# First batch by the casting software queue, four of its masks as copy and select, its last k scaled on POOL

## The chip, the cores and the metric

One core of a Trainium2 chip. The metric is device microseconds (us) of an execution. Before the change it was 208.72 us, the median of 3 runs (208.58 to 209.14). A ratio is the mean time of one kernel's fast runs over the mean time of the other's from the same rounds on the same chip, so it is not quite the ratio of the medians that are quoted beside it.

PE is the matrix engine, PEld its weight loads, DVE the vector engine, ACT the scalar engine, POOL the GpSimd engine and SP the engine that issues the hardware queue's transfers. L400 is line 400 of the kernel that the profile is of; the line numbers differ from kernel to kernel.

## The reference

```python
# q, k, v: (4, 8, 768, 64), float32
for t in range(S):                                   # retention, per batch and head
    state = gamma * state + outer(k[t], v[t])
    y[t] = scale * q[t] @ state
x = y.transpose(0, 2, 1, 3).reshape(B, S, H * D)     # (4, 768, 512)
h = np.maximum(x.transpose(0, 2, 1) @ w_tok1, 0.0) @ w_tok2
u = x + h.transpose(0, 2, 1)                         # token mixing
out = u + np.maximum(u @ w_ch1, 0.0) @ w_ch2         # channel MLP
```

## The kernel before

Each batch has four head pairs. The front of a pair loads k, q and v (384 KB of float32 each), scales k and casts q and v to float16, transposes k and q on PE, computes the attention of chunks of 128 in two halves, masks it, adds the state, and does the token mixing. The back of a batch is the channel MLP. The weights are cast on their way by the software queue (POOL): two for the token mixing, then the first channel weight in two pieces, c1a and c1b, then the second channel weight, c2.

```python
# loads: all by the hardware queue, and batch 1 waits for c1b
dma = nc.sync.dma_start(out=t, in_=rows.rearrange("h (c p) d -> p (h c) d", p=P))
if b == 1:
    tc.add_manual_dep(dma.ins, wops["c1", 1].ins.ins.name, ...,   # [cut]
                      reason="the weights come first")
# ... k scaled on DVE, q and v cast on POOL ...
nc.vector.tensor_scalar(k16[:, :, j, :], src, gk[:, h:h + 1], None, ALU.mult)
nc.gpsimd.tensor_copy(t.rearrange("p c h d -> p h c d"), src.tile...)   # [cut]
# ... attention of one half into two PSUM banks, then the mask ...
nc.vector.tensor_tensor(am, src[:, :HC], mask, ALU.mult)
```

The order of the work is not the order of this text. A list scheduler in the kernel (`arrange`) simulates all engines with assumed durations, and the instructions of each engine are emitted in the order that it finds. PE executes them in that order, whatever is ready.

PSUM has eight banks, five for `fa` tiles and three for `ba` tiles. A bank is free when its last reader has read it: for an attention half the reader is the mask on DVE.

Of the kernel before, what the change touches and what calls it, by code (L numbers as in the profile page):

```python
# [17 lines left out]
def kernel(  # L18
# [13 lines left out]
    P = 128  # L32
# [42 lines left out]
    make_identity(nc, ident16)  # L75

    gp = const_p.tile([P, NP], FP, name="gp")
    for p in range(NP):
# [4 lines left out]
    nc.gpsimd.affine_select(  # L83
        out=mask, in_=mask, compare_op=ALU.is_ge, fill=0.0,
        base=0, pattern=[[0, HC], [1, P]], channel_multiplier=-1,
    )
# [12 lines left out]
    BUFS = dict(kf=4, qf=4, vf=4, k16=3, q16=3, v16=4, kT=4, qT=4, U=3, am=8, x16=2, h1=4, u16=3, u16w=2,  # L99
# [3 lines left out]
    LONG, XK, XQ, XU, XBAR, RING = 2, 2, 2, 2, 1500, 3  # L103
# [18 lines left out]
    def arrange():  # L122


        way = {}
        for op in reversed(ops):
            if op.first is not None:
                way[op] = way.get(op, 0) + op.lat + SEM
                for d in op.deps:
                    way[d] = max(way.get(d, 0), way[op])  # L130
        for op in ops:
            if op.first is not None:
                op.prio = (op.prio[0], 0, EARLY * op.first - way[op], op.first)
        free = dict(PE=5000, ACT=5000, DVE=4600, POOL=4000, SP=1300, DMA=1300)
        taken = {t: [] for t in BUFS}
        todo, order, ring = list(ops), [], []
        while todo:
            best = []
            for op in todo:
                if any(d.end is None for d in op.deps):  # L140
                    continue
                start = free[op.eng]
                if op.dma and op.eng == "SP" and len(ring) >= RING:
                    start = max(start, ring[-RING])
                for d in op.deps:
                    if d.eng == op.eng and (d.dma or d.eng == "PE"):
                        continue
                    start = max(start, d.end + (30 if d.eng == op.eng else SEM) + op.guard)
                more = {}
                for s in op.takes:  # L150
                    q = taken[s.tag]
                    n = len(q) + more.get(s.tag, 0) - BUFS[s.tag]
                    more[s.tag] = more.get(s.tag, 0) + 1
                    if n >= 0:
                        old = q[n]
                        if any(u.end is None for u in old.users):
                            break
                        start = max([start] + [u.end + SEM for u in old.users])
                else:
                    best.append((start, op))  # L160
            t = min(b[0] for b in best)

            eng = min(best, key=lambda b: (b[0], b[1].prio))[1].eng
            start, op = min((b for b in best if b[1].eng == eng and b[0] <= t + 20),
                            key=lambda b: b[1].prio)
            free[op.eng] = start + op.occ
            op.start = start
            if op.dma:
                free["DMA"] = max(free["DMA"], start + 50) + op.dma
                op.end = free["DMA"] + 1600  # L170
                if op.eng == "SP":
                    ring.append(free["DMA"])
            else:
                op.end = start + op.lat
            for s in op.takes:
                taken[s.tag].append(s)
            todo.remove(op)
            order.append(op)
        return order
# [16 lines left out]
    def weight(key, ns, out, src, dep):  # L196
        def emit():
            return nc.gpsimd.dma_start(out=out, in_=src.rearrange("(i p) j -> p i j", p=P))
        wops[key] = Op("POOL", (0,) if key in ("t1", "t2", ("c1", 0)) else (1, 0, 99), 800, 800, emit, deps=[dep], dma=ns)


    load_done = [None]
# [4 lines left out]
    def front(b, p):  # L207
# [20 lines left out]
        sl, ld = {}, {}  # L228
        for nm, src in (("k", k), ("q", q), ("v", v)):
            sl[nm] = Slot(nm + "f")  # L230

            def emit(nm=nm, src=src):
                t = tile_of(sl[nm], sb, [P, 2 * NC, D], FP)
                rows = src[b, 2 * p:2 * p + 2]
                if nm == "q" and b < LONG:

                    dma = nc.sync.dma_start(  # L237
                        out=t.rearrange("p (h f i) d -> p h f (i d)", h=2, f=2),
                        in_=rows.rearrange("h (f p i) d -> p h f (i d)", f=2, p=P))
                else:  # L240
                    dma = nc.sync.dma_start(out=t, in_=rows.rearrange("h (c p) d -> p (h c) d", p=P))  # L241
                if b == 1:
                    tc.add_manual_dep(
                        dma.ins, wops["c1", 1].ins.ins.name,
                        mybir.DependencyInfo(mybir.DependencyClass.Sync, mybir.DependencyReason.DATA),
                        reason="the weights come first")
            ld[nm] = Op("SP", (0, b, p), 100, 100, emit,
                        deps=[load_done[-1]] + ([wops["c1", 1]] if b == 1 else []),
                        takes=[sl[nm]], dma=1200 if nm == "q" and b < LONG else 1750)
            load_done.append(ld[nm])  # L250

        K, Q, V = Slot("k16"), Slot("q16"), Slot("v16")

        def emit():
            k16 = tile_of(K, sb, [P, NC, 2, D], F16)
            for j in range(2):
                h = 2 * p + j
                src = sl["k"].tile[:, j * NC:(j + 1) * NC, :]
                if KENG == "ACT":
                    nc.scalar.mul(k16[:, :, j, :], src, gk[:, h:h + 1])  # L260
                else:
                    nc.vector.tensor_scalar(k16[:, :, j, :], src, gk[:, h:h + 1], None, ALU.mult)  # L262
        KENG = "DVE"
        kc = op(KENG, 900, 980, emit, [ld["k"]], [K], [sl["k"]])

        def cast(slot, src):
            def emit():
                t = tile_of(slot, sb, [P, NC, 2, D], F16)
                nc.gpsimd.tensor_copy(t.rearrange("p c h d -> p h c d"),  # L269
                                      src.tile.rearrange("p (h c) d -> p h c d", h=2))  # L270
            return emit
        qc = op("POOL", 770, 830, cast(Q, sl["q"]), [ld["q"]], [Q], [sl["q"]])
        vc = op("POOL", 770, 830, cast(V, sl["v"]), [ld["v"]], [V], [sl["v"]])
        KT, QT = Slot("kT"), Slot("qT")

        def turn(src, dst, dep, eng):
            T = Slot("fa")

            def emit():
                T.tile = tp = tile_of(T, ps, [P, 512], FP).bitcast(F16)  # L280
                for c in range(NC):
                    nc.tensor.transpose(tp[:, c * P:(c + 1) * P],  # L282
                                        src.tile[:, c].rearrange("p h d -> p (h d)"), ident16)
# [11 lines left out]
        def crossbar(src, dst, dep):  # L295
            def emit():
# [3 lines left out]
                    in_=src.tile.rearrange("p c h d -> p (c h d)"))  # L300
# [7 lines left out]
        def emit():  # L308
            st = tile_of(ST, ps, [P, 512], FP)
            for c in range(NC - 1):  # L310
                for j in range(2):
                    nc.tensor.matmul(st[j * D:(j + 1) * D, c * D:(c + 1) * D], K.tile[:, c, j],  # L312
                                     V.tile[:, c, j], start=True, stop=True)
# [20 lines left out]
        def emit():  # L334
            nc.vector.tensor_scalar(RS.tile[D:, :, D:], US.tile[D:], g128[2 * p + 1], None, ALU.mult)
        r1 = op("DVE", 400, 480, emit, [prev, r0], [], [US, RS])
# [4 lines left out]
        for hf in range(2):  # L341
# [12 lines left out]
            for j in range(2):  # L354
                def emit(hf=hf, j=j, A=A):
                    am = tile_of(AM[2 * hf + j], sb, [P, HC, P], F16)
                    src = A[j].tile.rearrange("p (i t) -> p i t", t=P)
                    nc.vector.tensor_tensor(am, src[:, :HC], mask, ALU.mult)  # L358
                am_ops.append(op("DVE", 470, 550, emit, [a], [AM[2 * hf + j]], [A[j]]))
        X16 = Slot("x16")  # L360
        x_ops, xf = [], []
        for hf in range(2):
            Y = Slot("fa")

            def emit(hf=hf, Y=Y):
                y = tile_of(Y, ps, [P, 512], FP)
                R = RS.tile
                for i in range(HC):
# [5 lines left out]
                    for j in range(2):  # L374
                        nc.tensor.matmul(o[:, j * D:(j + 1) * D], AM[2 * hf + j].tile[:, i],  # L375
                                         V.tile[:, c, j], start=(c == 0), stop=(c == 0 or j == 1))
# [51 lines left out]
        t1 = op("PE", 690, 860, emit, x_ops + [wops["t1"], None if first else t2_done.get(b * NP + p - 1)], [T1], [X16])  # L428
# [10 lines left out]
        for hf in range(2):  # L439
# [9 lines left out]
            t2 = op("PE", 350, 520, emit, [hr, wops["t2"]], [T2], [H1])  # L449
# [64 lines left out]
    def back(b):  # L514
# [6 lines left out]
        for sh in range(2):  # L521
# [26 lines left out]
            for i in range(HC):  # L548
# [3 lines left out]
                for part in range(parts):  # L552
# [25 lines left out]
                    op("SP", 100, 100, emit, [ad], [], [O]).dma = 800 // parts  # L578


    weight("t1", 2000, wt1, moe_w_tok1, None)
    weight("t2", 2000, wt2, moe_w_tok2, None)
    for i, (f0, f1) in enumerate(CUT1):
        weight(("c1", i), 650 * (f1 - f0), wc1[i], moe_w_ch1[:, f0 * P:f1 * P], None)
    weight(("c2", 0), 7800, wc2, moe_w_ch2, None)
    casts = [front(0, p) for p in range(NP)]
    after = {"t1": casts[2][2], ("c1", 0): casts[3][1]}
    last = None
    for key, o in wops.items():
        o.deps += [d for d in (after.get(key), last) if d is not None]  # L590
        last = o

    for b in range(1, B):
        for p in range(NP):
            front(b, p)
    for b in range(B):
# [40 lines left out]
```

## Time and profile before

| kernel before | |
|---|---|
| time, median | 208.72 us |
| profiled span | 206.8 us |
| first channel matmul (end of the head) | 38.08 us |
| PE busy from there to the last matmul | 164.83 of 165.22 us |
| padding matmuls, all in the head | 62 |

### The profile page before, as it was taken

To read this page: it belongs to the slowest core of one execution; us is meant where nothing else is said; L and a number is where in the kernel's file an instruction comes from. 1 tells how busy PE (TensorE), PEld (TensorE's weight loads), DVE (VectorE), ACT (ScalarE), POOL (GpSimd) and SP (SyncE) were. 2 spreads that over 40 slices of the span, in tenths; PEclk is the share of its full clock that TensorE was granted. 3 is DMA by queue.
4 is the path that set the end of the run, shared out by engine and by line. 5 is a ranking of instruction groups with operands and counts; after the bars stand their busy time and mean duration, and the time that the engine had idled before them with its cause. 6 is when DMAs were issued, how large, how long until landed. Compare 5 with 4: busy or idle time off the path is not lost.

```text
span 206.8 us, 4738 instructions
## 1 busy us (share of the span) xinstructions
PE 198.9 (96%) x1898; PEld 120.5 (58%) x1898; DVE 114.8 (56%) x291; ACT 96.2 (47%) x205; POOL 61.9 (30%) x107
## 2 busy tenths in 40 slices
PE   6899899999999999999999999999999999999993
PEld 2554487564667667576656574458556545545552
DVE  6377896114998878996794726686663021021021
ACT  7237458674497842455502670176215604604600
POOL 2338852113345635252533134115311000000000
PEclk9999999999999999999999999999999999999999
DMA  6999999999999999989995899996722012012012
GB/s 165 248 244 247 188 207 201 202 263 237 295 271 213 189 203 230 226 177 162 212 171 141 145 216 218 155 263 107 152 101 75 17 51 101 3 51 101 0 54 101
DMA packets 92790, 34.13 MB, mean 165 GB/s; under 512 B 81888, under 2 KB 89312, under 8 KB 92768
## 3 DMA queue, kind: packets, MB, share of 16 engines
q1 hardware_dynamic: 89104, 29.89, 72.6%
q0 software_dynamic: 3664, 3.93, 11.4%
q8 instruction: 15, 0.25, 0.5%
q14 instruction: 7, 0.06, 0.1%
HBM read 26.74 MB, written 6.29 MB: 160 GB/s over the span
## 4 chain that ended last, share of the span: by engine, by line
PE 83%; SPq 5%; DMA 4%; DVE 3%; ACT 2%; issue 1%; POOL 0%; DVEq 0%
PE ba L532 31%; PE ba L561 29%; PE fa L426 4%; DMA kf<-in_k_dram 4%; PE fa L447 4%; PE fa L351 3%; SPq L241 3%; PE fa L375 3%; SPq L237 2%; PE fa L372 2%; PE fa L282 2%; PE fa L312 2%; DVE k L262 1%; PE ba L426 1%; PE ba L189 1%
## 5 line engine op out<-in xcount | busy, mean ns | idle before, releaser
L532 PE MATMUL ba<-uT,wc 128*128 128x384 f16 x384 | 68.4, 326 | 0.0
L561 PE MATMUL ba<-wc,h 128*128 128x512 f16 (+1 forms) x300 | 67.7, 371 | 0.0
L545 ACT ACTIVATE h<-ba 128x384 f16<-128x384 f32 x96 | 46.7, 490 | 41.3 <-PE ba L532 40.4
L532 PEld LDWEIGHTS <-wc 128*128 128x128 f16 x384 | 35.5, 98 | 22.2
L570 DVE TENSOR_TENSOR o<-x,ba 128x512 f32<-128x512 f32 (+1 forms) x25 | 16.6, 663 | 50.1 <-PE ba L561 49.7
L561 PEld LDWEIGHTS <-h 128*128 128x128 f16 x300 | 27.6, 98 | 27.0
L358 DVE TENSOR_TENSOR am<-fa,mask 128x384 f16<-128x384 f32 x64 | 32.7, 550 | 5.3 <-PE fa L351 4.8
L403 POOL CAST x<-x 128x384 f16<-128x384 f32 x30 | 15.0, 512 | 37.6 <-issue 20.4
L269 POOL CAST q<-qf 128x768 f16<-128x768 f32 x16 | 13.7, 854 | 29.3 <-DMA qf<-in_q_dram 24.7
L386 ACT ACTIVATE x<-fa,gy 128x192 f32<-128x192 f32 (+1 forms) x42 | 15.1, 417 | 9.2 <-PE fa L375 8.7
L262 DVE TENSOR_SCALAR k<-kf,gk 128x384 f16<-128x384 f32 x32 | 14.5, 495 | 7.6 <-DMA kf<-in_k_dram 7.5
L189 PE MATMUL fa<-zero 128*128 128x512 f16 x54 | 15.9, 425 | 2.4 <-DVE zero L52 1.3
L331 ACT ACTIVATE r<-U 64x320 f16<-64x320 f32 x16 | 7.4, 465 | 23.2 <-DVE U L324 23.2
L324 DVE SCALAR_TENSOR_TENSOR U<-U,gp,fa 128x64 f32<-128x64 f32 x64 | 17.1, 275 | 1.0
L454 DVE TENSOR_TENSOR x<-x,fa 128x384 f32<-128x384 f32 x24 | 12.5, 549 | 6.3 <-POOL q L269 3.1
L291 ACT COPY qT<-fa 128x768 f16<-128x768 f16 x8 | 11.6, 1455 | 6.5 <-PE fa L282 6.5
L269 POOL CAST v<-vf 128x768 f16<-128x768 f32 x16 | 13.2, 827 | 4.6 <-DMA vf<-in_v_dram 3.7
L375 PE MATMUL fa<-v,am 128*128 128x64 f16 x192 | 13.9, 193 | 0.0
L375 PEld LDWEIGHTS <-am 128*128 128x128 f16 x192 | 12.1, 98 | 1.9
L426 PEld LDWEIGHTS <-wt 128*128 128x128 f16 x192 | 11.7, 98 | 2.6 <-issue 0.4
L447 PEld LDWEIGHTS <-wt 128*128 128x128 f16 x192 | 11.8, 98 | 2.0
L465 POOL CAST u16w<-x 128x384 f16<-128x384 f32 x16 | 7.9, 506 | 14.7 <-DVE x L454 14.6
(53 smaller groups left out, 164.3 us busy)
## 6 DMA issues: line engine op xcount, KB each, us to landing
kf<-in_k_dram SPq DMA_DIRECT2D x16, 384.0 KB, 6.5
qf<-in_q_dram SPq DMA_DIRECT2D x16, 384.0 KB, 6.1
vf<-in_v_dram SPq DMA_DIRECT2D x16, 384.0 KB, 5.8
out_dram<-o SPq DMA_DIRECT2D x23, 256.0 KB, 2.3
wc<-in_moe_w_ch_dram POOLq DMA_DIRECT2D x1, 1536.0 KB, 18.9
wc<-in_moe_w_ch_dram POOLq DMA_DIRECT2D x1, 1024.0 KB, 11.7
wt<-in_moe_w_tok_dram POOLq DMA_DIRECT2D x2, 384.0 KB, 6.9
wc<-in_moe_w_ch_dram POOLq DMA_DIRECT2D x1, 512.0 KB, 7.3
```

The source lines that it names most:

```text
L189: nc.tensor.matmul(slot.tile, zero[:, :P], zero, start=True, stop=True)
L262: nc.vector.tensor_scalar(k16[:, :, j, :], src, gk[:, h:h + 1], None, ALU.mult)
L269: nc.gpsimd.tensor_copy(t.rearrange("p c h d -> p h c d"), src.tile.rearrange("p (h c) d -> p h c d", h=2))
L324: nc.vector.scalar_tensor_tensor(U[:, c], U[:, c - 1], gp[:, p:p + 1], o, ALU.mult, ALU.add)
L358: nc.vector.tensor_tensor(am, src[:, :HC], mask, ALU.mult)
L375: nc.tensor.matmul(o[:, j * D:(j + 1) * D], AM[2 * hf + j].tile[:, i], V.tile[:, c, j], start=(c == 0), stop=(c == 0 or j == 1))
L426: nc.tensor.matmul(acc[:, jt * P:(jt + 1) * P], wt1[:, i, jt * P:(jt + 1) * P], X16.tile[:, i], start=(i == 0), stop=(i == NC - 1))
L447: nc.tensor.matmul(acc[:, i * P:(i + 1) * P], wt2[:, jt, t], H1.tile[:, jt], start=(jt == 0), stop=(jt == NJ - 1))
L532: nc.tensor.matmul(acc[:, :SH], w[:, ct, f * P:(f + 1) * P], UT.tile[:, ct, sh * SH:(sh + 1) * SH], start=(ct == 0), stop=(ct == NP - 1))
L545: nc.scalar.activation(H2.tile[:, ft], A.tile[:, :SH], AF.Relu)
L561: nc.tensor.matmul(A.tile[:, :CW], H2.tile[:, ft, i * P:(i + 1) * P], wc2[:, ft, cs], start=(ft == 0), stop=(ft == NF - 1))
L570: nc.vector.tensor_tensor(o[:, :CW], X.tile[:, sh * HC + i, cs], A.tile[:, :CW], ALU.add)
```

## The change

The intent is to shorten the loading of batch 0: q and v are cast on the way, so POOL casts nothing for this batch; of its twelve loads only the first k stays on the hardware queue. Four of its sixteen masks go from DVE to an ACT copy and a POOL select, and its last k is scaled on POOL. All batches after the first load as before. The scheduler now has a model of two queues that share the transfer rate.

```diff
+    RING = dict(SP=3, POOL=8)
+    ASIDE, RACT = ((1, 1), (1, 3), (2, 1), (2, 3)), ()
+    KPOOL = (3,)
@@ scheduler, transfers
-                free["DMA"] = max(free["DMA"], start + 50) + op.dma
-                op.end = free["DMA"] + 1600
+                mine, other = op.eng + "ring", ("POOL" if op.eng == "SP" else "SP") + "ring"
+                at = max(free[mine], start + 50)
+                both = max(0, free[other] - at)
+                shared = min(op.dma, both // 2)
+                free[mine] = at + op.dma + shared
+                free[other] += shared
+                op.end = free[mine] + 1600
@@ loads
+                eng = nc.gpsimd if first and p else nc.sync
...
+        def cast(slot, nm):
+            if first:
+                ...
+                    return nc.gpsimd.dma_start(out=t, in_=rows.rearrange("h (c p) d -> p (h c) d", p=P))
@@ k scaling
-                    nc.vector.tensor_scalar(k16[:, :, j, :], src, gk[:, h:h + 1], None, ALU.mult)
+                (nc.gpsimd if keng == "POOL" else nc.vector).tensor_scalar(
+                    k16[:, :, j, :], src, gk[:, h:h + 1], None, ALU.mult)
+        keng = "POOL" if first and p in KPOOL else "DVE"
@@ q of batch 0 is transposed per head: 12 transposes a pair, not 6
+                    if src is Q and first:
+                        for j in range(2):
+                            nc.tensor.transpose(tp[j * D:(j + 1) * D, c * P:(c + 1) * P],
+                                                src.tile[:, j * NC + c], ident16)
@@ mask
-                    nc.vector.tensor_tensor(am, src[:, :HC], mask, ALU.mult)
+                    if off:
+                        nc.scalar.copy(am, src[:, :HC])
+                    else:
+                        nc.vector.tensor_tensor(am, src[:, :HC], mask, ALU.mult)
...
+                        nc.gpsimd.affine_select(
+                            out=M.tile, in_=M.tile, compare_op=ALU.is_ge, fill=0.0,
+                            base=0, pattern=[[0, HC], [1, P]], channel_multiplier=-1)
```

(Cut: the order in which POOL issues the transfers, index changes for the new layout of q and v, a fourth q16 buffer, and the output stores' priority.)

## The prediction

> **What bounds the kernel now.** I read the page first (busy shares and slices), then the chain in order of time, then the timeline of DVE and of the SP queue around the first loads of batch 1, then the DMA queues in short windows.
>
> ```profile
> PE 198.9 (96%) x1898; PEld 120.5 (58%) x1898; DVE 114.8 (56%) x291; ACT 96.2 (47%) x205; POOL 61.9 (30%) x107
> ```
>
> ```profile
> 0.00:38.08 38.08, 34.11 (x388) 20.85 (x389) 26.49 (x86) 21.55 (x48) 18.77 (x35) 1.00 1.16 214
> 38.08:203.30 165.22, 164.83 (x1512) 99.62 (x1510) 87.90 (x205) 74.65 (x158) 43.18 (x72) 1.00 0.79 156
> ```
>
> ```profile
> 12.24 7.61 DMA kf<-in_k_dram
> 19.88 0.76 DVE k L262 x2
> ...
> 38.08 7.80 PE ba L532 x48
> 45.88 0.43 PE ba L561 x2
> 46.31 0.34 PE fa L282 x6
> ...
> 203.26 0.42 DVE o L570
> ```
>
> The second fence gives PE, PEld, DVE, ACT, POOL busy time, clock, DMA share and GB/s in two stretches. Up to 38.08 us ("the head") batch 0 is loaded and its attention and token mixing run; PE's busy time there holds 62 matmuls on a zero tile, which are only padding. From 38.08 us on PE works 164.83 of 165.22 us: the end is the end of the head plus a fixed 165 us. In the head the chain goes over the loads (the last k lands about 19.8) and then over a nearly full PE. Two places at the border of the head matter for this change:
>
> ```profile
> 34.56 0.37 SPq L241 DMA_DIRECT2D kf<-in_k_dram  x1
> ```
>
> ```profile
> 44.23 0.75 DVE L262 TENSOR_SCALAR k<-kf,gk 128x384 f16<-128x384 f32 x2 [7.20 <-DMA kf<-in_k_dram]
> ```
>
> Batch 1's first k is issued at 34.56, because it waits for the second piece of the first channel weight (c1b), and is usable at 44.23: 9.67 us, against 3.9 at the very start. The queues say why (DMA windows 36 to 37, then 40 to 41 us; packets, MB written, share):
>
> ```profile
> q0 software_dynamic: 201, 0.21, 123.1%
> ```
>
> ```profile
> q0 software_dynamic: 151, 0.15, 90.1%
> q1 hardware_dynamic: 159, 0.04, 30.6%
> ```
>
> The second channel weight (c2, 1536 packets) is already in the software queue. First it runs alone, then one of its packets goes for each packet of k, so that k (1536 packets) is done when c2 is. Now it costs nothing: PE has 7.80 + 0.43 us of channel matmuls to do before the first k transposes, and those ran at 46.31.
>
> **What the Trainium skill says.** "DMA: Bandwidth & Descriptors", Queues, rings and completion order: each engine takes turns between queues packet by packet; the 151 against 159 packets agree. The same page, Why small descriptors are slow: a fixed three cycles or so per packet, 32 bytes per cycle; with its 850 MHz a 2 KB packet would take about 79 ns, and 201 packets per us over 16 engines are 80 ns, which agrees. Its Specifications table warns of read-modify-write below 512 B; no run here yet shows casts that write 128 B. "TensorE: Matmul & The Clock Gate", Part 1: some 3.4 us of idling halve the clock. The first eight padding matmuls take 3.60 us, 0.45 each, against 0.22 later, so the trace shows a cold array.
>
> **The change part by part.**
>
> Loads. q and v of batch 0 (eight loads) and three of four k go by the software queue; q and v are cast on the way, so POOL loses eight casts of 0.83 us. Now: k and v take about 1.7 us each, q 1.4 (the landings of a pair repeat every 4.85 us), 19.2 in all. The software queue alone reads float32 at twice 0.20 MB/us, some 400 GB/s, with packets that read 2 to 4 KB; the new ones read 256 B (v, k) or 768 B (q). By 11 and 27 cycles a packet, 13 and 32 ns, a v (96 packets per engine) is at least 1.24 us and a q (32) 1.02; I take 1.3 and 1.1 (the diff's scheduler assumes 1.4 and 1.2), and 1.6 for an uncast k. Sum: 1.7 + 3x1.6 + 4x1.3 + 4x1.1 = 16.1 us, 3.1 less.
>
> POOL issues 15 DMAs before its first other work on batch 0 apart from the identity and the mask; from the ninth on each waits for the DMA eight before it. With eight in flight the queue doesn't run dry. That POOL is blocked until c1b is issued (when the third q lands, about 14 us) hurts nobody: its first selects are wanted then.
>
> Elementwise work. DVE loses four masks (0.47 us apart) and one k scaling of 0.75, 2.6 us of 26.5 in the head. ACT gets four copies, about 0.4 to 0.5 each, POOL four selects of 0.5 and two scalings of about 0.5. Both have room (21.6 and 18.8 us of 38). PE gets 24 transposes more (a q chunk per head instead of per pair), 0.34 us per pair.
>
> End of the head, M. In the new PE order the last q's transposes come before batch 0's third attention. They ran at 22.17; with q landing near 18 and no cast, at about 18. What stands behind them: four t1 of 0.67 and eight t2 halves of 0.34, 5.4; transposes of u 1.35; four attention halves 1.1; state 0.3; outputs 1.5; k transposes 0.3: 10 us, and 13 padding matmuls of 0.22, 2.8. So 18 + 0.7 + 12.8 = 31.5 with no wait; the same stretch now holds about 13 us of work in 15.9, so I add 2: M = 33.5, 4.6 us earlier than 38.08.
>
> Batch 1's first k. Its load still waits for c1b. First packet at 2.2 us as now, loads 16.1, the weights up to c1b 4.72 MB of float32 at 410 GB/s 11.5, completion 0.9: c1b lands at L = 30.7 (this sum for the kernel now gives 33.8; it is 34.5). So L comes only about 3.8 us earlier, as the weights' share of the stream is unchanged. c2 is again in the queue behind c1b, so k is usable at L + 9.67 = 40.4 and scaled at L + 10.42 = 41.1; with the hand-over to PE 41.2.
>
> And PE's order has moved. The new scheduler lets two queues share time for the length of the shorter load (about 3.5 us of transfer for k), so it puts k's transposes after 28 of the 48 first channel matmuls, not after 48 and two more: M + 28x0.1625 = 33.5 + 4.55 = 38.05. PE executes in order and stands still from 38.05 to 41.2, 3.1 us. From the transposes on everything is as now: 165.2 - 4.55 = 160.6 us to the last matmul, which then ends at 201.8 instead of 203.26. The gain of 4.6 becomes 1.4. A standstill of this length may make the array cold for part of 3.4 us, up to 1.7 us; I take 0.4. Gain 1.0: 208.72 - 1.0 = 207.7, which I round towards the possibility of a milder wait: **207.5 us**.
>
> **The rivals.**
>
> 1. The head's gain arrives whole. Then 204.1, just above 2%. For it: PE is saturated after the head, and the tail of batch 0 surely moves forward. Against it: 9.67 us for one k beside c2, and a PE order that leaves it only 4.55 us after M. It needs k to overtake c2.
> 2. Casts with short writes are slow (read-modify-write). At 2.2 us per v, 1.5 per q and 1.7 per k the loads take 21.6 us, L = 36.2, the transposes wait until 46.7 and the end comes at 207.3: about 4 us slower, 212.7. Against it: the weights are cast in the same queue without loss, and the per-packet cost seen so far is small. No trace of short casts speaks for either.
> 3. POOL becomes the bound of the head: the skill ("SBUF — State Buffer", Who interferes with whom) says that GpSimd and DVE's two-port operations lock each other out, descriptor writing included. DVE's k scalings are such candidates, but they are 0.75 us per pair. I expect single delays below 0.5 us: 208 at most.
>
> **Range and chances.** The gain is the smaller of 38.08 - M and about 32.1 - L. M is 32 to 36, L 29 to 33.5, so the second governs: from 3 us gained to 1.5 lost, with the cold clock on top. Range 205.2 to 210.0. Over 2% faster (below 204.55) needs L below 28 or rival 1: 0.12. Over 2% slower (above 212.9) needs rival 2: 0.06. Within 2%: 0.82.
>
> **What would show it.** Right: the first channel matmuls start at 32 to 36 us; PE then has an idle of 2 to 4 us in front of batch 1's first k transposes, put down to DVE's k scaling, which itself waits for the DMA of kf; that load takes 9 to 10 us from issue to use; c2 and k alternate packet for packet. The v casts land 1.2 to 1.5 us apart from their predecessors, and c1b at 29 to 33. Wrong: no such idle (rival 1), or the last k landing after 20 us (rival 2), or POOL's selects as releaser of the last outputs (rival 3).

## More of the kernel before

Where the scheduler expects PE to stand idle in the head, it inserts matmuls on a zero tile, to keep the array busy. Their number is fixed when the kernel is built, and they write into the PSUM bank that the next operation is about to take:

```python
def tile_of(slot, pool, shape, dtype, tag=None):
    slot.tile = pool.tile(shape, dtype, name=tag, bufs=BUFS[tag])
    if pool is ps:
        for _ in range(idle[0]):                       # padding
            nc.tensor.matmul(slot.tile, zero[:, :P], zero, start=True, stop=True)
        idle[0] = 0
    return slot.tile
...
idle[0] = max(0, int((o.start - end - 40) / (220 if end > 1500 else 500)))
```

The lines are the timeline of PE and then of DVE of the kernel before (start, duration, engine, line, operation, tiles, count; in brackets the idle time ahead and what ended it):

```profile
10.18 3.61 PE L189 MATMUL fa<-zero 128*128 128x512 f16 x16 [0.53 <-DVE am L358]
13.63 0.50 PE L282 MATMUL fa<-ident,q 128*128 128x128 f16 x6
```

```profile
9.57 0.56 DVE L358 TENSOR_TENSOR am<-fa,mask 128x384 f16<-128x384 f32 x1
10.04 0.74 DVE L262 TENSOR_SCALAR k<-kf,gk 128x384 f16<-128x384 f32 x2
```

After the first attention, sixteen padding matmuls stand ahead of the second pair's q transposes. They wait 0.53 us for a bank that the first mask releases, and then take 0.226 us each. On DVE the first mask comes ahead of the second pair's k scaling.

## The result

The changed kernel took 211.46 us (median of 4 runs, 210.56 to 211.59) against 208.68 us for the kernel before (4 runs, 208.58 to 209.14). The ratio is 1.012, 95% interval 1.0087 to 1.0152. So it is slower by about 1.2%, within the 2% that counts as the same, but outside the predicted range of 205.2 to 210.0.

The page of the changed kernel, first the busy line, then the costliest groups' row of the padding (time busy, mean ns, then idle ahead and what ended most of it):

```profile
PE 198.8 (95%) x1912; PEld 120.3 (57%) x1912; DVE 112.5 (54%) x285; ACT 98.0 (47%) x209; POOL 70.5 (34%) x116
```

```profile
L193 PE MATMUL fa<-zero 128*128 128x512 f16 x46 | 15.6, 477 | 5.3 <-DVE am L413 2.0
```

DVE lost 2.3 us of work as intended, and PE is as busy as before. But the 46 padding matmuls ahead of `fa` tiles take 15.6 us and have 5.3 us of idle time ahead of them.

Windows of the changed kernel up to and behind the end of its head (PE, PEld, DVE, ACT, POOL busy, granted clock, DMA share, GB/s):

```profile
0.00:41.94 41.94, 34.12 (x402) 20.84 (x403) 25.70 (x82) 22.79 (x52) 27.18 (x44) 0.96 1.29 198
41.94:206.40 164.46, 164.46 (x1512) 99.50 (x1510) 86.34 (x203) 75.17 (x158) 43.28 (x72) 1.00 0.72 146
```

The head ends at 41.94 instead of 38.08 (predicted: 33.5). Behind it PE works without a gap, as before. So the whole loss lies in the head. There the chain of what ended last names the padding; the pieces are start, duration, what (the second is the last q's transposes):

```profile
12.31 3.79 PE fa L193 x9
...
25.45 0.47 PE fa L325 x12
```

The timelines of DVE and of PE at the padding:

```profile
10.33 1.27 DVE L310 TENSOR_SCALAR k<-kf,gk 128x384 f16<-128x384 f32 x2
...
11.71 0.54 DVE L413 TENSOR_TENSOR am<-fa,mask 128x384 f16<-128x384 f32 x1
```

```profile
9.81 0.51 PE L400 MATMUL fa<-qT,kT 64*128 64x128 f16 x12
12.31 3.79 PE L193 MATMUL fa<-zero 128*128 128x512 f16 x9 [1.99 <-DVE am L413]
16.03 0.53 PE L325 MATMUL fa<-ident,q 128*64 128x128 f16 x12
```

And the window around it:

```profile
10.00:15.00 5.00, 3.01 (x19) 1.25 (x14) 3.82 (x10) 0.47 (x1) 5.00 (x7) 0.74 1.69 214
```

The new schedule puts the second pair's k scaling ahead of the first mask on DVE. That k had landed by 9.4 (issued at 3.91, 5.5 us from issue to landing), so the scaling did not wait for its load here: it began at 10.33, right behind DVE's earlier work. It took 1.27 us, where it takes 0.74 before, so the first mask ended at 12.27. Only then was a bank free for the nine padding matmuls. PE stood still for 1.99 us, and then did the nine at half speed, 0.42 us each (the granted clock in that window is 0.74). The padding was meant to fill such a wait. It stood behind the wait instead, and was added to it. The last q's transposes, which I had put at 18, ran at 25.4. It is not the load that held them: that q was issued at 11.04 and landed 7.3 us later, at 18.3.

One thing that I predicted did not show: batch 1's first k transposes. DVE has its k at 41.07, as foretold (41.1), but PE is so late that it does not have to wait.

```profile
41.07 1.00 DVE L310 TENSOR_SCALAR k<-kf,gk 128x384 f16<-128x384 f32 x2 [0.20 <-DMA kf<-in_k_dram]
```

```profile
41.77 4.71 PE L594 MATMUL ba<-uT,wc 128*128 128x384 f16 x28
46.32 0.50 PE L329 MATMUL fa<-ident,k 128*128 128x128 f16 x6
```

### The profile page after: what moved, and what is told of

Its sections match the earlier page's. It is cut to its first block, busy times and chain, and to the rows that moved or that the text cites. A ratio compares the mean times of both kernels' runs of the same rounds, so it can differ in the third digit from the quotient of the medians.

```text
span 209.9 us, 4758 instructions
## 1 busy us (share of the span) xinstructions
PE 198.8 (95%) x1912; PEld 120.3 (57%) x1912; DVE 112.5 (54%) x285; ACT 98.0 (47%) x209; POOL 70.5 (34%) x116
## 4 chain that ended last, share of the span: by engine, by line
PE 90%; ACT 4%; DMA 2%; DVE 2%; issue 1%; POOL 0%; POOLq 0%; ACTq 0%
PE ba L594 30%; PE ba L623 30%; PE fa L193 5%; PE fa L509 4%; PE fa L488 4%; PE fa L400 3%; PE fa L437 3%; ACT qT L337 2%; DMA q<-in_q_dram 2%; PE fa L434 2%; PE fa L329 2%; PE fa L358 2%; PE fa L325 1%; PE ba L509 1%; PE ba L488 1%
## 5 line engine op out<-in xcount | busy, mean ns | idle before, releaser
L594 PE MATMUL ba<-uT,wc 128*128 128x384 f16 x384 | 69.2, 326 | 0.0
L607 ACT ACTIVATE h<-ba 128x384 f16<-128x384 f32 x96 | 46.8, 491 | 38.9 <-PE ba L594 38.2
L413 DVE TENSOR_TENSOR am<-fa,mask 128x384 f16<-128x384 f32 x60 | 30.9, 550 | 15.7 <-PE fa L400 15.4
L465 POOL CAST x<-x 128x384 f16<-128x384 f32 x30 | 15.3, 518 | 38.2 <-issue 18.6
L193 PE MATMUL fa<-zero 128*128 128x512 f16 x46 | 15.6, 477 | 5.3 <-DVE am L413 2.0
L310 DVE TENSOR_SCALAR k<-kf,gk 128x384 f16<-128x384 f32 x30 | 13.6, 493 | 0.2 <-DMA kf<-in_k_dram 0.2
L527 POOL CAST u<-x 128x384 f16<-128x384 f32 x16 | 7.9, 509 | 15.4 <-DVE x L516 15.4
L434 PE MATMUL fa<-r,qT 128*128 128x128 f16 x80 | 12.2, 220 | 0.0
```

Source lines behind the costliest of these rows:

```text
L434: nc.tensor.matmul(o, QT.tile[:, c * P:(c + 1) * P], R[:, c - 1], start=True, stop=False)
L527: nc.gpsimd.tensor_copy(u, X.tile[:, half(hf), pc])
L594: nc.tensor.matmul(acc[:, :SH], w[:, ct, f * P:(f + 1) * P], UT.tile[:, ct, sh * SH:(sh + 1) * SH], start=(ct == 0), stop=(ct == NP - 1))
L607: nc.scalar.activation(H2.tile[:, ft], A.tile[:, :SH], AF.Relu)
```

## The experiments

The theory after the result: padding that is bound to a bank waits for the late first mask, lets the array go idle and cold, and then still has to be executed; this hides the wait for batch 1's k that I had predicted. Rivals: the padding is simply too much PE work; the elementwise parts of the change (masks on ACT and POOL, k on POOL) delay the head; the delay is that of the loads.

The twelve kernels were all correct. "Before" in the table is the kernel before in the same rounds. The first eight experiments ran on one chip, the last four on another.

| run | time, median (lowest to highest) | before | ratio, 95% | head ends |
|---|---|---|---|---|
| a_nopad | 207.63 (206.84 to 208.09) | 208.76 | 0.9934 (0.9901 to 0.9968) | 37.0 |
| b_nopad | 210.17 (210.06 to 210.43) | 208.76 | 1.0062 (1.0036 to 1.0088) | 39.9 |
| a_no9 | 208.54 (207.85 to 209.92) | 208.76 | 0.999 (0.9941 to 1.004) | 38.2 |
| a_spare | 207.27 (207.1 to 207.57) | 208.76 | 0.9923 (0.9892 to 0.9953) | 35.8 |
| a_swap | 208.15 (207.4 to 209.26) | 208.8 | 0.9978 (0.9928 to 1.0029) | 37.7 |
| a_masks | 210.32 (209.33 to 211.27) | 208.8 | 1.0067 (1.0015 to 1.0119) | 39.5 |
| a_k3dve | 210.55 (209.94 to 211.97) | 208.8 | 1.0088 (1.0041 to 1.0134) | 40.4 |
| a_spare_early | 207.57 (207.18 to 209.21) | 208.8 | 0.9958 (0.9904 to 1.0011) | 36.4 |
| b_spare | 208.42 (208.16 to 209.28) | 208.85 | 0.9992 (0.9974 to 1.0009) | 38.1 |
| a_spare_kq | 206.57 (206.27 to 207.39) | 208.85 | 0.9905 (0.9888 to 0.9923) | 36.7 |
| a_ss | 207.58 (206.86 to 208.11) | 208.85 | 0.9941 (0.9922 to 0.9959) | 36.3 |
| a_ss_kq | 206.33 (206.14 to 206.92) | 208.85 | 0.9889 (0.9875 to 0.9904) | 36.4 |

(The head's end is the start of the first channel matmuls in PE's timeline, which lies up to 0.2 us ahead of the chain's start for the same group. It is of the one profiled run of each kernel: for a_nopad the fastest of its runs, for a_no9, a_swap and a_masks one of the two faster, for b_nopad and b_spare the slowest. All the ratios are within 2%; what is compared here are smaller differences, by their intervals.)

### The padding taken away: a_nopad, b_nopad, a_no9

In the first two all padding behind the first group is dropped, from the changed kernel and, as a control, from the kernel before. In the third only the fourth group goes, the nine.

```diff
                 idle[0] = max(0, int((o.start - end - 40) / (220 if end > 1500 else 500)))
+                if idle[0]:
+                    idle[0] = idle[0] if group == 0 else 0      # a_no9: 0 if group == 3 else idle[0]
+                    group += 1
```

> The changed kernel with all padding matmuls after the first six taken out, nothing else moved. Theory 1 (the padding, a fixed number of matmuls in PE's order, now stands on the path): the head ends 4 to 9 us earlier (33 to 38 instead of 41.9), after which batch 1's first k, usable at about 41, becomes the wait; the time falls to 206.5 to 208. Theory 2 (the elementwise engines and the PSUM banks bound the head, padding only fills waits): 211.4 within 0.5. Theory 3 (the padding keeps the array at full clock): slower, 213 or more, with transposes of 0.85 us per twelve instead of 0.47.

> Control: the kernel before with all padding after the first eight taken out. Its chain holds about 3 us of padding in the head. Theory 1: 206 to 207.5. Theory 2: 208.7 within 0.5. Theory 3 (clock): 210 or more.

> The changed kernel without one group of padding alone, the nine matmuls ahead of the second pair's q transposes, which took 3.79 us at half speed. Theory 1: 2 to 3.8 us faster, 207.6 to 209.5. Theory 2: the same as the changed kernel within 0.5. Theory 3: the transposes behind the gap run at half speed and little is won, 210.5 to 212.

Without padding the changed kernel gains 3.8 us and the kernel before loses 1.4. So in the kernel before the padding is worth having (my theory 1 had expected a gain there, and missed; it came out as theory 3 has it), and in the changed kernel it costs. Yet a_nopad's head ends at 37.0 only. Its array is cold for long stretches: the granted clock is 0.50 to 0.53 from 7.5 to 17.5 us. The timeline of PE in a_nopad:

```profile
12.03 0.85 PE L325 MATMUL fa<-ident,q 128*64 128x128 f16 x12 [2.42 <-DVE am L413]
```

The transposes themselves now wait for the late mask, 2.42 us, and run at half speed (0.85 us for twelve, against 0.53 us warm), as the attention ahead of them did. In a_no9, which keeps the other padding, the array is warm ahead of the wait:

```profile
11.29 0.85 PE L325 MATMUL fa<-ident,q 128*64 128x128 f16 x12 [2.09 <-DVE am L413]
```

The wait is 2.09 us and the half speed behind it is the same; by the medians the nine alone are worth 2.9 us. The wait for the mask is thus there without any padding; the padding adds to it.

### The wait taken from the padding: a_spare, b_spare

The count of padding matmuls and the order of everything stay. Only the bank that the padding ahead of `fa` tiles writes is another: a `ba` bank that no one reads, until the first `ba` tile is wanted.

```diff
             for _ in range(idle[0]):
-                nc.tensor.matmul(slot.tile, zero[:, :P], zero, start=True, stop=True)
+                nc.tensor.matmul(spare[0] if tag == "fa" and spare[0] is not None else slot.tile,
+                                 zero[:, :P], zero, start=True, stop=True)
+            if tag == "ba":
+                spare[0] = None
```

> The changed kernel with as much padding, but that of the attention part written to a bank that nobody waits for, so that it starts at once (at 10.3 instead of 12.3 us in the second pair) and the array has no gap of 2 us. If the loss is the wait for a bank plus the half clock after it: 207.5 to 209. If the loss is the number of padding matmuls itself: no better than 210.5.

> Control: the kernel before, same number of padding matmuls, but those in front of an fa tile write to a spare bank that nobody waits for. Theory A (what the spare bank cures is the changed kernel's own stall: nine padding matmuls stood behind the release of a bank by the first mask, idled the array and ran at half speed): the kernel before has no such stall, its padding costs 2.9 us in its chain warm and cannot run ahead of the bank for long, so 207.8 to 208.9. Rival (the write to the next op's bank is a general loss of about 1.5 to 4 us in either kernel): 206 to 207.

The changed kernel gains 4.2 us by this, the kernel before nothing that the runs can show (0.9992, interval 0.9974 to 1.0009). PE in a_spare, same place:

```profile
9.72 0.51 PE L405 MATMUL fa<-qT,kT 64*128 64x128 f16 x12
10.16 2.12 PE L195 MATMUL ba<-zero 128*128 128x512 f16 x9
12.30 0.53 PE L330 MATMUL fa<-ident,q 128*64 128x128 f16 x12
...
20.58 0.53 PE L330 MATMUL fa<-ident,q 128*64 128x128 f16 x12
```

The nine run while DVE is still busy, at 0.24 us each, and the second pair's q transposes start at 12.30 instead of 16.03. The last q's transposes start at 20.58 instead of 25.38, 4.8 us earlier. Of these the changed kernel's timeline shows 3.0 as idle time in front of padding (1.99 here, then 0.15, 0.20 and 0.67) and 1.7 as half speed (3.79 less 2.12). In these two profiled runs that is the loss ahead of the last q, all but 0.1 us of it (not every run of the changed kernel has the half speed: see a_masks below). It is not the amount of padding, and not the loads: both are the same.

Cured of this, the changed kernel's head is 2.1 us shorter than that of the kernel before (35.8 against 37.9 in the same view, and 38.1 in b_spare): this is what the change was worth there. And with the head's end at 35.8, the wait that I had predicted is there. The chain of a_spare, and PE's timeline:

```profile
15.16 16.27 DMA wc<-in_moe_w_ch_dram
...
31.50 9.67 DMA kf<-in_k_dram
...
41.20 0.76 DVE k L315 x2
```

```profile
35.82 4.71 PE L599 MATMUL ba<-uT,wc 128*128 128x384 f16 x28
42.01 0.51 PE L334 MATMUL fa<-ident,k 128*128 128x128 f16 x6 [1.47 <-DVE k L315]
```

The chain is now c1b, then k's load of 9.67 us, then DVE's scaling, as in the prediction: 6 us of gain at the head's end (41.8 to 35.8) became 4.2 us of time.

### What makes the first mask late: a_swap

On DVE the second pair's k scaling is moved behind the first three masks. The padding still writes into the next operation's bank.

```diff
-    for o in arrange():
+    seq = arrange()
+    seq.remove(marks[0, 1, "k"])
+    seq.insert(seq.index(marks[0, 0, "am", 0]) + 1, marks[0, 1, "k"])
+    for o in seq:
```

> The changed kernel with one move on DVE: the scaling of the second k (its load lands at 10.1 us) goes behind the first three masks instead of ahead of them; padding as in the changed kernel. Theory A (the scaling waits for a software-queue load and holds back the mask that frees the bank for the nine padding matmuls; PE then stands idle for 2 us and goes on at half speed): the nine start near 10.8 instead of 12.3 and take 2.0 instead of 3.8 us, 2 to 3.5 us off, 208 to 209.5. Theory B (the number of padding matmuls is too large in any case, the wait is not the cause): 1 us or less, 210.5 or more.

```profile
9.30 0.55 DVE L414 TENSOR_TENSOR am<-fa,mask 128x384 f16<-128x384 f32 x1
```

```profile
9.90 2.10 PE L193 MATMUL fa<-zero 128*128 128x512 f16 x9 [0.75 <-DVE am L414]
11.93 0.53 PE L326 MATMUL fa<-ident,q 128*64 128x128 f16 x12
```

The mask now comes at 9.30 instead of 11.71, the idle time in front of the nine is 0.75 us instead of 1.99, the array stays at full speed, and the time falls by 3.3 us against the changed kernel's 211.46. Not all of the 2.41 us of the mask is due to the move: in this run the array was warm from its first transposes on (twelve in 0.53 us at 5.87, against 0.85 at 5.74), so the first attention ran at 8.64 instead of 9.81. The fair partner is a_no9's run, as warm and with the old order on DVE: attention at 8.69, mask at 10.69, idle 2.09 us. So the order on DVE is what released the bank late, by 1.4 us. (A wait for the scaling's load, which the expectation names, is 0.27 us in a_no9 and none in the changed kernel.) It also shows that this one place is not all: later padding still waits, and the head ends 1.9 us later than in a_spare.

### The elementwise parts undone: a_masks, a_k3dve

The order of all work stays as the changed kernel has it; only the instruction differs. In a_masks the four masks are DVE multiplications again, in a_k3dve the last k is scaled on DVE.

```diff
-                        nc.scalar.copy(am, src[:, :HC])
+                        nc.vector.tensor_tensor(am, src[:, :HC], mask, ALU.mult)       # a_masks
...
-                (nc.gpsimd if keng == "POOL" else nc.vector).tensor_scalar(
+                nc.vector.tensor_scalar(                                               # a_k3dve
```

> The changed kernel with its four masks on DVE again in place of the ACT copies and POOL selects, order and padding unchanged. If this part carries the loss (ACT copies stand ahead of other ACT work, POOL selects late): 208.5 to 210. If it is off the path: 211.4 within 0.7. If it helps as meant: 212 or more.

> The changed kernel with the last k of batch 0 scaled on DVE again. On POOL it took 2.48 us for two where I had put 1.0, but the transposes of that k ran only at 29.4 us, 6 us after it was ready. If it is off the path as the trace suggests: 211.4 within 0.7. If it matters: 210 or less.

Their ratios to the kernel before, 1.0067 and 1.0088, have intervals that overlap that of the changed kernel (1.0087 to 1.0152), so neither is shown to help, nor to do nothing: both medians fall between the times that I had expected for either outcome. The single times of a_masks fall in two groups (209.33 and 209.48, 211.16 and 211.27), and its profiled run was one of the fast group:

```profile
12.30 2.10 PE L193 MATMUL fa<-zero 128*128 128x512 f16 x9 [1.44 <-DVE am L413]
```

Here the nine began at the same time as in the changed kernel, 12.30, but ran at full speed, after an idle of 1.44 us. Between these two profiled runs that alone is 1.7 us. It does not explain the scatter of the times, though. The record has the mean granted clock of every run, and a half-speed stretch that loses 1.7 of 209.9 us takes it to 0.992 (an estimate), as in the changed kernel's profiled run. That kernel's run of 211.34 has 1.0, and was no faster for it than the three with 0.992; the two slow runs of a_masks have 1.0 as well. Only in a_k3dve do the two slower runs have 0.992 and the two faster ones 1.0 and 0.999. So the half speed is part of the loss where 0.992 shows it, the profiled run among them, and not in every run. What takes its place in the others stays open, since only one run of each kernel has a trace. How long the array stays cold at the start also differs by run (see a_swap), and the granted clock reads 1.00 there either way; no run tests whether that is it.

POOL's k scaling was mis-sized by me (2.48 us for two instructions, I had taken 1.0), but the k transposes wanted it only at 29.6 in the changed kernel, and it ended at 22.8.

### The wait for batch 1's k: a_spare_early, a_spare_kq

Both build on a_spare. In the first, batch 1's loads wait for c1a and not for c1b, and are issued 4.9 us earlier on the hardware queue. In the second, batch 1's first k is put into the software queue itself, between c1b and c2; each engine's order of work is otherwise unchanged.

```diff
-                        dma.ins, wops["c1", 1].ins.ins.name,
+                        dma.ins, wops["c1", 0].ins.ins.name,                  # a_spare_early
```

```diff
-                eng = nc.gpsimd if first and p else nc.sync
+                eng = nc.gpsimd if first and p or (b, p, nm) == (1, 0, "k") else nc.sync
-                if b == 1:
+                if b == 1 and (p, nm) != (0, "k"):
...
+    seq.remove(marks["kb1"])                                                 # a_spare_kq
+    seq.insert(seq.index(wops["c2", 0]), marks["kb1"])
```

> The version with padding in a bank nobody waits for, and batch 1's loads waiting for the first piece of the first channel weight instead of the second. There the head ends at 35.9, and PE idles 1.47 us for the k that is usable only at 41.2. If that wait is what is left of the loss: k usable at 32 to 36, no idle, the time 1.2 to 1.8 us below that version, 205.4 to 206.2. If the earlier loads hold back the weights by as much as they gain: 207 to 208.

> The changed kernel with the spare bank, and the first k of batch 1 put into the software queue between c1b and c2 (it is written behind c1b by the order of the queue), each engine's order of work otherwise unchanged. Theory: k then lands about 1.7 us behind c1b, near 33 us instead of 41, the idle of 1.47 us in front of batch 1's first k transposes goes, and the time falls from 207.3 to 205.6 to 206.2; q of batch 1 is issued first on the hardware queue and is usable near 40 to 41.5, wanted at about 42.4. Rival (the wait moves to q, which now stands alone beside c2, or c2 itself becomes late): 206.8 to 207.5, with an idle in front of the q transposes or of the first wc2 matmuls.

The first is a miss: no gain at all (207.57 against a_spare's 207.27), which is the outcome that I had set against the theory. Its chain:

```profile
26.57 14.72 DMA kf<-in_k_dram
```

Issued 4.9 us earlier, k took 14.72 us instead of 9.67 and was usable at 41.32, as late as before. The DMA queues of a_spare_early in the window 31 to 32 us, and of a_spare 38 to 39 (packets, MB, share):

```profile
q0 software_dynamic: 150, 0.15, 90.3%
q1 hardware_dynamic: 147, 0.04, 28.2%
```

```profile
q1 hardware_dynamic: 525, 0.16, 72.2%
q0 software_dynamic: 82, 0.08, 46.5%
```

Beside a filled software queue the hardware queue gets one packet for each of the other's, about 150 in a us, and k has 1536 packets, so an estimate from these is 10.2 us. In a_spare_early its packets began to flow in the window 30 to 31, some 3.7 us after the issue, and 30.3 + 10.2 is 40.5. In a_spare they began only at about 35, but then c2 ran out and the rate rose to 525 and, from 40 to 41, to 828 packets a us. Both ways k lands near 41: what decides is when the software queue's bytes ahead of and beside it are gone, not when k is issued. Why the first packet comes so long after the issue stays open.

The second does what the theory says. Its PE timeline:

```profile
36.67 4.71 PE L601 MATMUL ba<-uT,wc 128*128 128x384 f16 x28
41.22 0.50 PE L336 MATMUL fa<-ident,k 128*128 128x128 f16 x6
...
43.18 0.50 PE L336 MATMUL fa<-ident,q 128*128 128x128 f16 x6
```

No idle time ahead of the k transposes, and none ahead of the q transposes, which the rival had expected. The time, 206.57, is somewhat above what I expected; in the profiled run the head ended 0.85 us later than in a_spare's, and why is not shown. The intervals of the two ratios overlap (a_spare 0.9892 to 0.9953, this 0.9888 to 0.9923; they are from different rounds), so this pair alone does not prove the gain in time; the next pair does.

### Both waits together: a_ss, a_ss_kq

a_ss is a_spare with a_swap; a_ss_kq adds k in the software queue.

> Spare bank and the scaling of the second k moved behind the first three masks, together. Theory: head ends at 35 to 36 us, but the wait for batch 1's first k (usable about 42 whatever the head does) takes what is gained: 207.0 to 207.5, idle before the k transposes 1.5 to 3 us. Rival (the end follows the head's end alone): below 206.6.

> Spare bank, moved scaling, and batch 1's first k in the software queue ahead of c2. Theory: both waits gone, the end follows the head: 205.2 to 206.0, that is 1.3 to 1.7 per cent under the kernel before. Rival (another wait follows): 206.8 or more.

```profile
42.62 0.51 PE L335 MATMUL fa<-ident,k 128*128 128x128 f16 x6 [1.61 <-DVE k L315]
```

```profile
36.44 4.71 PE L603 MATMUL ba<-uT,wc 128*128 128x384 f16 x28
40.99 0.50 PE L337 MATMUL fa<-ident,k 128*128 128x128 f16 x6
```

The first line is a_ss, the other two a_ss_kq. Between these two, in the same rounds, only the place of one load differs. The head ends at 36.3 and 36.4, the idle time of 1.61 us goes, and the time falls from 207.58 to 206.33; the intervals (0.9922 to 0.9959 and 0.9875 to 0.9904) do not touch. This shows the second wait in time, not only in the trace. Moving the k scaling, which was worth 3.3 us by itself, is worth nothing beside the spare bank (a_ss 207.58, a_spare 207.27): both cure the same wait.

Both times are a little above what I had expected (207.0 to 207.5 and 205.2 to 206.0). a_ss_kq is the best version that was run by its median, 1.1% under the kernel before and 5.1 us under the changed kernel; a_spare_kq's interval overlaps its own.

## Why the prediction was wrong, point by point

- **The fixed tail.** Right. 164.46 us of PE work from 41.94 to 206.40 with no gap, 165.2 before.
- **Loads and c1b, L = 30.7.** Right. SP issued batch 1's first k, which waits for c1b, at 31.38. Rival 2, slow casts with short writes, is not seen.
- **Batch 1's k usable at L + 9.67, its scaling at 41.1.** Right: 41.07. The 9.67 us even came out as the same number in a_spare. The packets alternate as said.
- **The order of PE, k transposes after 28 channel matmuls, and an idle of 2 to 4 us there.** The mechanism was right, but in the changed kernel nothing of it shows, as M + 4.55 = 46.5 lies behind 41.2. With the head cured it is there: 1.47 us in a_spare, 1.61 in a_ss. a_spare then took 207.27 against the predicted 207.5, although its M is 35.8 and not 33.5: as long as M + 4.55 lies ahead of 41.2, the wait takes up what M is late. So this part of the prediction held, and it is M alone that carried the time out of the range.
- **"End of the head, M = 33.5".** This is the step that failed: M was 41.94. It has two halves. The one from the last q's transposes to the end of the head, 15.5 us in my sum (33.5 less 18), held: 16.4 in the changed kernel (25.38 to 41.77, with 1.09 us of idle time ahead of six padding matmuls), 15.2 in a_spare and 15.5 in a_ss_kq. The other, "with q landing near 18 and no cast, at about 18", did not. I let the data decide when these transposes run, and q did land at 18.3. But PE executes a fixed order, and ahead of them stand the work of three pairs and 33 padding matmuls in eight groups, from 5.74 on. In the changed kernel this takes until 25.4; with the waits out of the padding it still takes until 20.6.
- So the miss of 8.3 us in M (41.77 less 33.5) is, in the profiled runs, 4.8 us of padding that waits for banks and runs cold ahead of the last q (25.38 less 20.58), 0.9 us behind it (16.4 less 15.5, where one group waits 1.09 us), and 2.6 us of work and padding in a fixed order that I did not add up (20.58 less 18).
- **"13 padding matmuls of 0.22".** I counted only those behind the last q and took them as warm and without a wait. The sixteen that wait 0.53 us in the kernel before, warm, were there to be read, with the mask that releases their bank. I did not ask what bank each group waits for, nor in what order DVE releases it.
- **"Elementwise work: both have room".** True of the sums, and POOL was no bound (rival 3). But the sum of DVE's work is not what PE waits for. A scaling of 0.74 us moved ahead of a mask and took 1.27 us. In the profiled run PE stood still for 1.99 us behind it and then lost 1.7 us to the half speed, more than the four masks taken from DVE (0.47 us each) could give.
- **The rivals.** Rival 1 (the gain arrives whole) did not come. None of the three was what happened, but the delays that rival 3 names may have had a part. In the changed kernel, a_spare, a_masks, a_k3dve, a_spare_early and a_spare_kq the two scalings began at times between 10.24 and 10.69, and ended at 11.58 to 11.60 every time, 0.5 us (the length of about one of them) behind the end of POOL's issue of a k load (10.03 to 11.09 in the changed kernel). This fits a lock held by POOL, of 0.53 us where I had allowed less than 0.5. It is argued: in a_swap they took 0.74 us at 10.88 beside the same issue, and no run isolates it.

## What to carry to other kernels

Filler work that keeps an engine warm should have no dependence of its own: give it a buffer that no one else waits for, or else it can stand behind the very wait that it should fill, and its time is added to it. Where there is no long wait to stand behind, as in the kernel before, this gains nothing (b_spare). When a scheduler fixes the order by modelled times, a change of one transfer's time re-orders every engine, so read the new order for what stands in front of each release, not only for the sums. And when a load shares the engines with a filled queue, its place in that queue is worth more than its time of issue.

## What the Trainium skill lacked or had wrong

- "TensorE: Matmul & The Clock Gate", Part 1: its table gives half speed after an idle window of some 3.4 us, free-running. Here a single idle time of 1.99 us (2.09 in a_no9) was followed by half speed, while 1.44 us and 1.23 us at the same place (a_masks, a_k3dve) were not. The half speed lasted some 3.4 us, from about 12.45 to 15.85 (an estimate from the granted clock of 0.99, 0.50 and 0.83 in the three windows of 2.5 us from 10.0 on), so the length agrees; but the 3.4 us ahead of it held some 1.3 us of PE work (up to 10.3), so the window was not idle throughout. The same Part tells of short idle times that make the clock swing, but gives no length for them.
- "DMA: Bandwidth & Descriptors": its Specifications' warning of read-modify-write below 512 B did not show as lost time for casting loads whose packets write 128 B (v) or 384 B (q): a pair of batch 0 (k, q and v) is loaded every 4.0 us, against 4.85 us uncast before, where k's and v's packets of 256 B are under the limit too. Its turns packet by packet are right (150 against 147), but it does not say what that makes of a load of 1536 packets of 256 B beside packets that write 1 KB (9.67 to 14.72 us), nor that the first packet beside a filled queue comes some 3.7 us after the issue.
- No page that I read has a time for scaling by a column on POOL: two of 128x384 took 2.48 us, against 0.74 us on DVE. In the changed kernel DVE's own took 1.27 us in a stretch in which POOL was busy issuing software-queue loads (5.00 of 5 us), in a_swap 0.74 us in the same stretch; no experiment here isolates that.
